# Block-causal attention and gated MLP on one core: the MLP over 9 blocks of 512 tokens in place of 16 half batches of 288

## The chip, the core and the metric

The kernel runs on one NeuronCore of a Trainium2 chip. The core has five engines that run side by side, each with its own queue that it works off in order: TensorE (PE in the profile; its weight loads are listed as PEld), VectorE (DVE), ScalarE (ACT), GpSimd (POOL) and SyncE (SP), which here issues the DMAs. Semaphores tie them together. SBUF is the working memory of 128 partitions; PSUM takes the results of TensorE, in banks of 2 KB a partition, which is 512 numbers in f32.

The metric is the time of one execution on the device in microseconds (us), less is better. Before the change it is 994.98 us, the median of three runs (994.43, 994.98, 995.88).

## The reference

What is computed, cut to what matters:

```python
# attention: batch 8, heads 8, sequence 576, head size 64
scores = (q @ k^T) / 8
scores = where(block_i >= block_j, scores, -1e9)     # blocks of 64 positions
attn = exp(scores - rowmax); attn = attn / (rowsum + 1e-9)
x = (attn @ v)  ->  [4608 tokens, 512]               # 8 batches x 576 tokens, heads side by side
# gated MLP without a nonlinearity
a = x @ w1                                           # 512 x 1024
b = x @ w2                                           # 512 x 1024
out = ((a * b) @ w3) @ w_out                         # 1024 x 1024, 1024 x 512
```

All inputs and the output are f32.

## The kernel before

**Work and tiling.** The 64 heads are worked off as 32 pairs (`n` from 0 to 31, four pairs to a batch; channel `c` of `x` is the pair's place in its batch). `pair(n)` computes attention for the two heads `j` of a pair and leaves `x` of that pair, transposed: 128 channels by 576 tokens. The products w3 @ w_out are taken once at the start, so the MLP is two products with w1 and w2 and one with the joined weight. Every operand of the MLP is split in a high and a low part (`w1h`/`w1l`, `xh`/`xl`, `gh`/`gl`) in the type fp32r, and a product is three matmuls: high x high, low weight x high, high weight x low.

**Stages.** In the first stage (pairs 0 to 3, `EARLY`) the weights are loaded, rebuilt from 64-bit words and split; attention of the first batch runs between these steps. Then the pool of that stage is closed, the pool `late` is opened over its memory, and pairs 4 to 31 run with the MLP of earlier batches woven in. After the last pair what is left of the MLP runs alone.

**The MLP before.** `gen_moe(b)` is a generator. For each half `h` of 288 tokens it goes over eight tiles `f` of the hidden size: 12 matmuls for `a`, 12 for `b`, both into PSUM tiles of the pool `ps_m` (two banks), then a copy of `a` by ACT, the product `g` by DVE, its high part by ACT and its low part by POOL. Then it goes over four tiles `e` of the output, 24 matmuls each, an ACT copy and an output DMA. Each `yield` ends a piece of 6 matmuls, so a batch has 96 pieces.

**The order.** TensorE's order is set by hand (`manual_schedule` for PE, from pair 4 on): the two strings of `PLAN`, one for each head, are worked off letter by letter. S is a tile of scores with its exponentials, V a piece of attention times v, M a piece of the row maxima of the next pair (`shift_mask`: casts, then six groups of matmuls with maxima on DVE, then a transpose), B and A the steps that split q and k (B for the second head of this pair, A for the first head of the next), R the row sums, N the taking of the result out of PSUM, T the division by the row sums, Q the split of v and the next load, F one piece of the MLP. Each pair has 24 F. `DELAY` is the number of F left out at the start of pair 4. The order on the other engines is left to the framework, which also adds the waits.

**Buffers that matter.** `raws` holds two buffers of 1792 numbers a partition, q, k and v of a pair together; `load(n + 2)` is called at the Q of the second head of pair `n`. `finish_x` splits each finished `x` at once into `xh` and `xl`, in halves of 288 tokens, in rotating buffers (eight in `xpool`, four in `late`); the subtraction for `xl` is on DVE for pairs 0 to 3 and on POOL later. Scores have two PSUM tiles (`ps_s`), the attention result one of two banks (`ps_x`), and the small products two (`ps_q`).

**Lines that the steps below speak of.** L182 are the mask matmuls `mx`, L186 their maxima, L233 the score matmuls, L248 and L249 the exponentials, L251 the low halves of the exponentials, L254 the row-sum additions on POOL, L296 attention times v, L309 the row sums' reduction `part`, L313 the small matmul `tot` that adds them over partitions, L160 the casts of q, k and v, L210 and L223 their low parts, L343 and L344 `xh` and `xl`, L392 the matmuls of `a` and `b`, L397 to L401 the steps of `g`, L408 the matmuls of the output, L412 and L413 its copy and DMA, L369 the product of the weights, L358 its low part, L96 the load of q, k and v.

Of the kernel before, what the change touches and what calls it, by code (L numbers as in the profile page):

```python
# [26 lines left out]
HALF = S // 2  # L27
RAW = 2 * S + 640
# [15 lines left out]
    "B F B S S F F B S S F F F F S M M F V V F V V F F R V F Q N F",  # L44
    "M A S F S F A S M F M S F F S M F A M V V V F F V V N Q R T M F F F",
# [7 lines left out]
DELAY = 3  # L53
# [5 lines left out]
def block_causal_attention__then__gated_mlp_kernel(ctx, tc, qkv, consts, ident_in, w1, w2, w3t, wout, out_t):  # L59
# [30 lines left out]
    raw_of = {}  # L90

    def load(n):
        t = raws.tile([P, RAW], F32, tag="raw", name=f"raw{n}")
        parts = (slice(S, 2 * S), slice(0, S), slice(2 * S, RAW)) if n == 0 else (slice(0, RAW),)
        for cols in parts:
            nc.sync.dma_start(out=t[:, cols], in_=qkv[n // NPAIR, n % NPAIR][:, cols])  # L96
        raw_of[n] = t

    load(0)
    nc.sync.dma_start(out=both, in_=ident_in)  # L100
    cst = raws.tile([P, RAW], F32, tag="raw", name="cst")
    nc.sync.dma_start(out=cst[0:D, 0 : 2 * S], in_=consts)
    for j in range(2):
        nc.vector.tensor_copy(qk[j][oth[j], 1::2, :], cst[0:D, 0 : 2 * S].rearrange("p (t s) -> p t s", t=2))
    nc.gpsimd.memset(qd, 0.0)

    tl = {}

    def open_early(pool):
        tl["early"] = pool  # L110
        tl["wo"] = pool.tile([P, NF, DM], F32, name="wo")

    def open_late():
# [4 lines left out]
        tl["pl"] = pool.tile([P, PW], F32R, name="pl")  # L118
# [45 lines left out]
    def shift_mask(n):  # L164
        r = raw_of[n]
        rqk = r[:, 0 : 2 * S].rearrange("p (t s) -> p t s", t=2)
# [34 lines left out]
    def prep_qk(n, j):  # L201
        rqk = raw_of[n][:, 0 : 2 * S].rearrange("p (t s) -> p t s", t=2)
# [10 lines left out]
    def prep_v(n, j):  # L213
        rv = raw_of[n][:, 2 * S :].rearrange("p (j c d) -> p j c d", j=2, c=5)[:, j]
# [10 lines left out]
    def s_tile(n, j, parts, p_early):  # L225
# [10 lines left out]
        for c, ks, at, q0, q1 in todo:  # L236
# [7 lines left out]
            if c == 0:  # L244
                p32 = rsum[:, q0:q1]
            else:
                p32 = tl["late"].tile([P, 448], F32, tag="p32", name=f"p{n}_{j}", bufs=2)[ks, 0:w]
# [76 lines left out]
    def take(n, j, xps, x32):  # L324
        o, x = own[j], oth[j]
        xl = tl["late"].tile([P, S], F32, tag="xlow", name=f"xlow{n}_{j}")
# [3 lines left out]
    def norm(n, x32, rr):  # L330
# [3 lines left out]
        nc.vector.tensor_tensor(out=x32, in0=x32, in1=rb, op=ALU.mult)  # L334

    def finish_x(n, x32):
        for h in range(2):
            at = (2 * n + h) % 12
            pool, bufs = (xpool, 8) if at < 8 else (tl["late"], 4)
            xh = pool.tile([P, HALF], F32R, tag="xh", name=f"xh{n}_{h}", bufs=bufs)  # L340
            xl = pool.tile([P, HALF], F32R, tag="xl", name=f"xl{n}_{h}", bufs=bufs)
            src = x32[:, h * HALF : (h + 1) * HALF]
            nc.scalar.copy(xh, src)  # L343
            (nc.vector if n < EARLY else nc.gpsimd).tensor_tensor(out=xl, in0=src, in1=xh, op=ALU.subtract)  # L344
            x_of[n // NPAIR, n % NPAIR, h] = (xh, xl)
# [35 lines left out]
    def gen_moe(b):  # L381
        mp, gh, gl = tl["late"], tl["gh"], tl["gl"]
        for h in range(2):
            for f in range(NF):
                acc = []
                for a, b2 in ((w1h, w1l), (w2h, w2l)):
                    t = ps_m.tile([P, 512], F32, tag="psm", name="ab")
                    fs = slice(f * P, (f + 1) * P)
                    for c in range(NC):
# [3 lines left out]
                        if c == 1 or (c == NC - 1 and len(acc) == 0):  # L393
                            yield
# [153 lines left out]
```

## Time and profile before

| what | value |
|---|---|
| three timed runs | 994.43, 994.98, 995.88 us |
| span of the profiled execution | 992.5 us |
| mean granted TensorE clock in it | 0.991 |
| first score matmul of pair 4 | 138.4 us |
| first MLP matmul | 142.1 us |
| last piece of the MLP woven into the pairs ends | about 912 us |
| last matmul starts | 988.5 us |
| moved by DMA over the span | 80.4 MB, 81 GB/s in the mean |

One execution is recorded by the hardware profiler, on the core's own clock. Its page gives the busy time of each engine, the span in 40 slices with one digit for the busy tenths of each, and the chain of work that ended last, followed back from the last instruction to what released it. Other views show the same record as groups of instructions by line, in order of time, or summed over windows. A matmul row such as `ab<-xh,w1h 128*128 128x288` names output and inputs, the size of the weight tile, and the moving tile (partitions x columns). Matmuls overlap in the pipeline: the duration of one is longer than the distance to the next, so the distance between starts is what to read. In an execution on one core there is no other core to disturb it.

### The profile page before, as it was taken

To read this page: it belongs to the slowest core of one execution; us is meant where nothing else is said; L and a number is where in the kernel's file an instruction comes from. 1 tells how busy PE (TensorE), PEld (TensorE's weight loads), DVE (VectorE), ACT (ScalarE), POOL (GpSimd) and SP (SyncE) were. 2 spreads that over 40 slices of the span, in tenths; PEclk is the share of its full clock that TensorE was granted. 3 is DMA by queue.
4 is the path that set the end of the run, shared out by engine and by line. 5 is a ranking of instruction groups with operands and counts; after the bars stand their busy time and mean duration, and the time that the engine had idled before them with its cause. 6 is when DMAs were issued, how large, how long until landed. Compare 5 with 4: busy or idle time off the path is not lost.

```text
span 992.5 us, 18182 instructions
## 1 busy us (share of the span) xinstructions
PE 960.8 (97%) x6624; PEld 879.1 (89%) x6624; DVE 695.6 (70%) x1316; ACT 557.2 (56%) x1433; POOL 535.6 (54%) x525
## 2 busy tenths in 40 slices
PE   4799979999999999999999999999999999999998
PEld 2355559999999999999999999999999999999998
DVE  7899997776777777777777777777767777774100
ACT  4656766555655556555655656665566555553221
POOL 0000027677675857676766767576776758572211
PEclk9799989999999999999999999999999999999999
DMA  7877622212222221211212222222122222100000
GB/s 239 260 256 233 196 62 63 54 57 74 62 68 80 63 85 51 85 54 47 72 59 77 63 86 62 74 62 60 52 74 65 65 81 62 49 13 25 7 19 25
DMA packets 36698, 80.40 MB, mean 81 GB/s; under 512 B 4416, under 2 KB 20928, under 8 KB 36608
## 3 DMA queue, kind: packets, MB, share of 16 engines
q1 hardware_dynamic: 36608, 79.23, 27.0%
q8 instruction: 52, 0.85, 0.3%
q14 instruction: 38, 0.31, 0.1%
HBM read 50.76 MB, written 9.44 MB: 61 GB/s over the span
## 4 chain that ended last, share of the span: by engine, by line
PE 83%; DVE 12%; DMA 2%; ACT 1%; issue 1%; SPq 0%; DVEq 0%; ACTq 0%
PE ab L392 38%; PE o L408 21%; PE s L233 10%; PE x L296 7%; PE mx L182 3%; PE w L369 3%; DVE m L186 2%; DVE qk L160 2%; DVE wbits L141 1%; DVE part L309 1%; DVE pl L251 1%; DMA raw<-in_qkv 1%; DVE qk L210 1%; PE tot L313 1%; DMA wraw<-in_w 1%
## 5 line engine op out<-in xcount | busy, mean ns | idle before, releaser
L254 POOL TENSOR_TENSOR rsum<-rsum,p 128x448 f32<-128x448 f32 x224 | 185.7, 829 | 135.9 <-ACT p L248 125.1
L401 POOL TENSOR_TENSOR gl<-g,gh 128x288 fp32r<-128x288 f32 x128 | 115.4, 902 | 114.5 <-ACT gh L400 110.2
L233 PE MATMUL s<-qk 128*128 128x288 f32 (+4 forms) x768 | 162.8, 317 | 13.8 <-DMA qk<-qk 4.6
L251 DVE TENSOR_TENSOR pl<-p,ph 128x448 fp32r<-128x448 f32 x168 | 138.8, 834 | 38.8 <-ACT ph L249 36.5
L392 PE MATMUL ab<-xh,w1h 128*128 128x288 f32 x512 | 158.7, 310 | 0.0
L408 PE MATMUL o<-gh,wh 128*128 128x288 f32 x512 | 155.3, 303 | 0.0
L392 PE MATMUL ab<-xh,w2h 128*128 128x288 f32 x512 | 154.0, 301 | 0.0
L392 PE MATMUL ab<-xl,w1h 128*128 128x288 f32 x512 | 151.5, 296 | 0.0
L392 PE MATMUL ab<-xh,w1l 128*128 128x288 f32 x512 | 151.4, 296 | 0.0
L408 PE MATMUL o<-gh,wl 128*128 128x288 f32 x512 | 151.1, 295 | 0.0
L392 PE MATMUL ab<-xh,w2l 128*128 128x288 f32 x512 | 151.0, 295 | 0.0
L392 PE MATMUL ab<-xl,w2h 128*128 128x288 f32 x512 | 150.9, 295 | 0.0
L408 PE MATMUL o<-gl,wh 128*128 128x288 f32 x512 | 150.8, 294 | 0.0
L210 POOL TENSOR_TENSOR qk<-raw,qk 64x1152 fp32r<-64x1152 f32 x54 | 144.1, 2668 | 2.0
L233 PEld LDWEIGHTS s<-qk 128*128 128x128 f32 (+1 forms) x768 | 114.9, 183 | 32.5 <-ACT pe L241 6.9
L186 DVE TENSOR_REDUCE m<-mx 128x1 f32<-128x512 f32 (+6 forms) x320 | 133.5, 452 | 10.6 <-PE mx L182 8.7
L223 POOL TENSOR_TENSOR vs<-raw,vs 128x320 fp32r<-128x320 f32 x56 | 49.7, 887 | 160.8 <-ACT vs L160 160.8
L249 ACT ACTIVATE ph<-s 128x288 fp32r<-128x288 f32 x336 | 130.7, 390 | 0.0
L399 DVE TENSOR_TENSOR g<-ab,a 128x288 f32<-128x288 f32 x128 | 58.2, 454 | 103.1 <-PE ab L392 66.6
L400 ACT CAST gh<-g 128x288 fp32r<-128x288 f32 x128 | 55.3, 432 | 110.7 <-DVE g L399 110.7
L248 ACT ACTIVATE p<-s 128x448 f32<-128x448 f32 x224 | 85.3, 381 | 50.8 <-PE s L233 36.1
L251 DVE TENSOR_TENSOR pl<-rsum,ph 128x288 fp32r<-128x288 f32 x112 | 60.4, 558 | 71.5 <-ACT ph L249 71.5
(70 smaller groups left out, 2136.9 us busy)
## 6 DMA issues: line engine op xcount, KB each, us to landing
raw<-in_qkv SPq DMA_DIRECT2D x31, 896.0 KB
qk<-qk SPq DMA_DIRECT2D x64, 288.0 KB
out_t<-o SPq DMA_DIRECT2D x64, 144.0 KB
wraw<-in_w3t SPq DMA_DIRECT2D x16, 512.0 KB
wraw<-in_w SPq DMA_DIRECT2D x16, 512.0 KB
wraw<-in_wout SPq DMA_DIRECT2D x8, 512.0 KB
qk<-ms SPq DMA_DIRECT2D x64, 2.2 KB
raw<-in_qkv SPq DMA_DIRECT2D x2, 288.0 KB
```

The costliest lines, as they stand in the source:

```text
L186: nc.vector.reduce_max(m[:, col : col + 1], sc, axis=AX.X)
L210: (nc.vector if n <= EARLY else nc.gpsimd).tensor_tensor(out=low, in0=rqk[o], in1=high, op=ALU.subtract)
L233: nc.tensor.matmul(t[ks, at : at + q1 - q0], qk[j][:, 2 + s, kr], qk[j][:, s, q0:q1], start=(s == 0), stop=(s == 1))
L248: nc.scalar.activation(p32, t[ks, at : at + w], AF.Exp, scale=SCALE)
L249: nc.scalar.activation(ph[ks, o : o + w], t[ks, at : at + w], AF.Exp, scale=SCALE)
L251: nc.vector.tensor_tensor(out=low, in0=p32, in1=ph[ks, o : o + w], op=ALU.subtract)
L254: nc.gpsimd.tensor_tensor(out=r, in0=r, in1=p32, op=ALU.add)
L296: nc.tensor.matmul(xps[:, to : to + w], v[:, c, :], parts[s][:, a : a + w], start=(u < 2 and s == 0), stop=((u, s) in ((0, 1), (len(PV) - ...
L392: nc.tensor.matmul(t[:, 0:HALF], l[:, c, fs], r, start=(c == 0 and s == 0), stop=(c == NC - 1 and s == 2))
L399: nc.vector.tensor_tensor(out=g32, in0=acc[1][:, 0:HALF], in1=a32, op=ALU.mult)
L401: nc.gpsimd.tensor_tensor(out=gl[:, f, :], in0=g32, in1=gh[:, f, :], op=ALU.subtract)
L408: nc.tensor.matmul(t[:, 0:HALF], l[:, f, es], r[:, f, :], start=(f == 0 and s == 0), stop=(f == NF - 1 and s == 2))
```

## The change

The MLP's unit becomes a block `k` of 512 tokens, counted over all 4608 tokens without regard to batches: 9 blocks, 96 pieces each, a piece being 3 matmuls of 512 columns. Block `k` takes tokens of batches `k - 1` and `k` (blocks 1 to 7), of batch 0 alone (block 0) or batch 7 alone (block 8); blocks 7 and 8 both need the last batch.

- `norm` multiplies `x` by the reciprocal row sums in two pieces, into f32 tiles per block and channel (`x_of[k, c]`, two buffers for each channel). `finish_x` is gone. `split_ready` splits a whole 512-token tile into `xh[c]` (ACT) and `xl[c]` (POOL), which have one buffer each; it is called when a pair is finished and when the last `f` of a block has been issued (`st["free"]`).
- In `gen_moe` the first `f` of a block takes the last channel last. `a * b` is written over `a32`; `o32` has one buffer.
- Raw inputs are two tiles, q and k (`rqk`) and v (`rv`). From pair 4 on each has one buffer. q and k of pair `n + 1` are loaded after the second B of pair `n`, v of pair `n + 2` at Q. Odd early pairs use the early pool, where the constants lie in the buffer that pair 1 takes after them.
- `PLAN`: the first head has one M less and one F more, the second one M more and one F less; `DELAY` is 6.
- Small tiles are cut: `pl`, two single buffers for `p32`, and `take` uses the tile `tr`.

```diff
-HALF = S // 2
-RAW = 2 * S + 640
+TB = 512
+NTB = NT // TB
+RQK, RV = 2 * S, 640
 PLAN = (
-    "B F B S S F F B S S F F F F S M M F V V F V V F F R V F Q N F",
-    "M A S F S F A S M F M S F F S M F A M V V V F F V V N Q R T M F F F",
+    "B F B S S F F B S S F F F F S M F F V V F V V F F R V F Q N F",
+    "M A S F S F A S M F M S F M S F M A M V V V F F V V N Q R T M F F F",
 )
-DELAY = 3
+DELAY = 6
...
-    raws = ctx.enter_context(tc.tile_pool(name="raws", bufs=2))
+    raws = ctx.enter_context(tc.tile_pool(name="raws", bufs=1))
-    xpool = ctx.enter_context(tc.tile_pool(name="xpool", bufs=8))
+    xpool = ctx.enter_context(tc.tile_pool(name="xpool", bufs=2))
...
+    def raw_pool(n):
+        return tl["early"] if n < EARLY and n % 2 else raws
+
+    def load_qk(n):
+        t = raw_pool(n).tile([P, RQK], F32, tag="rqk", name=f"rqk{n}")
+        for cols in (slice(S, 2 * S), slice(0, S)) if n == 0 else (slice(0, RQK),):
             nc.sync.dma_start(out=t[:, cols], in_=qkv[n // NPAIR, n % NPAIR][:, cols])
+        rqk_of[n] = t
+
+    def load_v(n):
+        t = raw_pool(n).tile([P, RV], F32, tag="rv", name=f"rv{n}")
+        nc.sync.dma_start(out=t, in_=qkv[n // NPAIR, n % NPAIR][:, RQK:])
+        rv_of[n] = t
...
-        tl["gh"] = pool.tile([P, NF, HALF], F32R, name="gh")
-        tl["gl"] = pool.tile([P, NF, HALF], F32R, name="gl")
+        tl["xh"] = [pool.tile([P, TB], F32R, name=f"xh{c}") for c in range(NC)]
+        tl["xl"] = [pool.tile([P, TB], F32R, name=f"xl{c}") for c in range(NC)]
+        tl["gh"] = pool.tile([P, NF, TB], F32R, name="gh")
+        tl["gl"] = pool.tile([P, NF, TB], F32R, name="gl")
...
-        nc.vector.tensor_tensor(out=x32, in0=x32, in1=rb, op=ALU.mult)
+        b, c = divmod(n, NPAIR)
+        for k in (b, b + 1):
+            lo, hi = max(k * TB, b * S), min((k + 1) * TB, (b + 1) * S)
+            if (k, c) not in x_of:
+                x_of[k, c] = xpool.tile([P, TB], F32, tag=f"x{c}", name=f"xr{k}_{c}")
+            sl = slice(lo - b * S, hi - b * S)
+            nc.vector.tensor_tensor(out=x_of[k, c][:, lo - k * TB : hi - k * TB], in0=x32[:, sl], in1=rb[:, sl], op=ALU.mult)
+        done_x.add((b, c))
+        split_ready()
+
+    def split_ready():
+        k = st["free"]
+        for c in range(NC):
+            if "xh" in tl and k < NTB and (min(k, B - 1), c) in done_x and (k, c) not in st["split"]:
+                st["split"].add((k, c))
+                src = x_of[k, c]
+                nc.scalar.copy(tl["xh"][c], src)
+                nc.gpsimd.tensor_tensor(out=tl["xl"][c], in0=src, in1=tl["xh"][c], op=ALU.subtract)
...
+    def gen_moe(k):
+        mp, xh, xl, gh, gl = tl["late"], tl["xh"], tl["xl"], tl["gh"], tl["gl"]
+        sides = ((w1h, w1l), (w2h, w2l))
+        for f in range(NF):
+            fs = slice(f * P, (f + 1) * P)
+            acc = [ps_m.tile([P, TB], F32, tag="psm", name="ab") for _ in sides]
+            order = [(i, c) for i in range(2) for c in range(NC)]
+            if f == 0:
+                order.sort(key=lambda ic: (ic[1] == NC - 1, ic))
+            for i, c in order:
+                a, b2 = sides[i]
+                for s, (l, r) in enumerate(((a, xh), (b2, xh), (a, xl))):
+                    nc.tensor.matmul(acc[i], l[:, c, fs], r[c], start=(c == 0 and s == 0), stop=(c == NC - 1 and s == 2))
+                if (i, c) == (0, NC - 1):
+                    a32 = mp.tile([P, TB], F32, tag="a32", name="a32", bufs=2)
+                    nc.scalar.copy(a32, acc[0])
+                if (i, c) != order[-1]:
+                    yield
+            nc.vector.tensor_tensor(out=a32, in0=acc[1], in1=a32, op=ALU.mult)
+            nc.scalar.copy(gh[:, f, :], a32)
+            nc.gpsimd.tensor_tensor(out=gl[:, f, :], in0=a32, in1=gh[:, f, :], op=ALU.subtract)
+            if f == NF - 1:
+                st["free"] = k + 1
+                split_ready()
+            yield
+        for e in range(DM // P):
+            t = ps_m.tile([P, TB], F32, tag="psm", name="o")
+            es = slice(e * P, (e + 1) * P)
             for f in range(NF):
+                for s, (l, r) in enumerate(((wh, gh), (wl, gh), (wh, gl))):
+                    nc.tensor.matmul(t, l[:, f, es], r[:, f, :], start=(f == 0 and s == 0), stop=(f == NF - 1 and s == 2))
+                if f < NF - 1:
+                    yield
+            o32 = mp.tile([P, TB], F32, tag="o32", name="o32")
+            nc.scalar.copy(o32, t)
+            nc.sync.dma_start(out=out_t[es, k * TB : (k + 1) * TB], in_=o32)
+            yield
...
                     elif step == "B":
                         fill(own_qk, 1)
+                        steps_b += 1
+                        if steps_b == 2 and n >= EARLY and not last:
+                            load_qk(n + 1)
...
-                        if j == 1 and n + 2 < NN:
-                            load(n + 2)
+                        if j == 1 and n + 2 <= EARLY:
+                            load_qk(n + 2)
+                        if j == 1 and n + 2 < NN and n + 1 != NPAIR:
+                            load_v(n + 2)
...
-    mlp = (None for b in range(B - 1) for _ in gen_moe(b))
+    mlp = (None for k in range(NTB) for _ in gen_moe(k))
     for n in range(NPAIR, NN):
         pair(n)
     fill(mlp, 1000)
-    fill(gen_moe(B - 1), 1000)
```

More of the change, by code (lines that the diff above doesn't have):

```diff
@@ L88, in block_causal_attention__then__gated_mlp_kernel, with open_early @@
     oth = [slice(D, P), slice(0, D)]
[L90 to L99, printed above, removed]
-    nc.sync.dma_start(out=both, in_=ident_in)
-    cst = raws.tile([P, RAW], F32, tag="raw", name="cst")
-    nc.sync.dma_start(out=cst[0:D, 0 : 2 * S], in_=consts)
+    tl = {}
+    rqk_of, rv_of = {}, {}
+    def raw_pool(n):
[3 more added lines that the diff above has]
+        for cols in (slice(S, 2 * S), slice(0, S)) if n == 0 else (slice(0, RQK),):
+            nc.sync.dma_start(out=t[:, cols], in_=qkv[n // NPAIR, n % NPAIR][:, cols])
+        rqk_of[n] = t
[3 more added lines that the diff above has]
+        rv_of[n] = t
+    load_qk(0)
+    load_v(0)
+    nc.sync.dma_start(out=both, in_=ident_in)
+    wstack = ExitStack()
+    wp = wstack.enter_context(tc.tile_pool(name="wp", bufs=1))
+    tl["early"] = wp
+    cst = wp.tile([P, RQK], F32, tag="rqk", name="cst")
+    nc.sync.dma_start(out=cst[0:D], in_=consts)
     for j in range(2):
-        nc.vector.tensor_copy(qk[j][oth[j], 1::2, :], cst[0:D, 0 : 2 * S].rearrange("p (t s) -> p t s", t=2))
+        nc.vector.tensor_copy(qk[j][oth[j], 1::2, :], cst[0:D].rearrange("p (t s) -> p t s", t=2))
     nc.gpsimd.memset(qd, 0.0)
[L107 to L111, printed above, removed]
+    def open_early():
+        tl["wo"] = wp.tile([P, NF, DM], F32, name="wo")
     def open_late():
@@ L201, in prep_qk @@
     def prep_qk(n, j):
-        rqk = raw_of[n][:, 0 : 2 * S].rearrange("p (t s) -> p t s", t=2)
+        rqk = rqk_of[n].rearrange("p (t s) -> p t s", t=2)
         o, x = own[j], oth[j]
@@ L246, in s_tile @@
             else:
-                p32 = tl["late"].tile([P, 448], F32, tag="p32", name=f"p{n}_{j}", bufs=2)[ks, 0:w]
+                p32 = tl["late"].tile([P, 448 if c % 2 else 320], F32, tag=f"p32{c % 2}", name=f"p{n}_{j}")[ks, 0:w]
             nc.scalar.activation(p32, t[ks, at : at + w], AF.Exp, scale=SCALE)
@@ L325, in take @@
         o, x = own[j], oth[j]
-        xl = tl["late"].tile([P, S], F32, tag="xlow", name=f"xlow{n}_{j}")
+        xl = work.tile([P, S], F32, tag="tr", name=f"xlow{n}_{j}")
         nc.scalar.copy(xl[o], xps[x, 384:960])
@@ L333, in norm @@
         nc.vector.transpose(rb, rr.unsqueeze(2).broadcast_to([P, S // 32, 32]))
-        nc.vector.tensor_tensor(out=x32, in0=x32, in1=rb, op=ALU.mult)
[L336 to L345, printed above, removed]
+        b, c = divmod(n, NPAIR)
[7 more added lines that the diff above has]
+        split_ready()
+    done_x = set()
+    st = {"free": 0, "split": set()}
+    def split_ready():
[6 more added lines that the diff above has]
+                nc.gpsimd.tensor_tensor(out=tl["xl"][c], in0=src, in1=tl["xh"][c], op=ALU.subtract)
     def gen_w(wp):
@@ L428, in block_causal_attention__then__gated_mlp_kernel @@
         prep_v(0, j)
-    load(1)
+    load_qk(1)
+    load_v(1)
     weights = gen_w(wp)
```

49 lines of the change are left out of this document (7 added, 42 removed).

## The prediction

> **What bounds the kernel now.** I read the page first (busy shares, the span in 40 slices, the chain that ended last by line), then the chain in order of time, then the windows of one pair of heads in the steady part.
>
> ```profile
> span 992.5 us, 18182 instructions
> ...
> PE 960.8 (97%) x6624; PEld 879.1 (89%) x6624; DVE 695.6 (70%) x1316; ACT 557.2 (56%) x1433; POOL 535.6 (54%) x525
> ...
> PE   4799979999999999999999999999999999999998
> ...
> DVE  7899997776777777777777777777767777774100
> ...
> PE 83%; DVE 12%; DMA 2%; ACT 1%; issue 1%; SPq 0%; DVEq 0%; ACTq 0%
> ```
>
> TensorE is busy 97% of the span and holds 83% of the chain; from the seventh slice to the last but one it never falls under nine tenths. VectorE has its nines only in the first six slices, 149 us (weights). The three timed runs (994.43 to 995.88, median 994.98) lie about 2.5 us over this span of 992.5; I take that as fixed, so the sum below is a change added to 994.98.
>
> A busy PE is pipelined, so what counts is the distance from one matmul to the next. The chain in order of time gives it: the last batch's MLP alone, and one row of the weight product.
>
> ```profile
> 52.93 6.87 PE w L369 x16
> ...
> 495.96 3.18 PE ab L392 x24
> ...
> 523.47 3.20 PE o L408 x24
> ...
> 912.48 25.28 PE ab L392 x192
> 937.76 12.80 PE o L408 x96
> 950.56 25.50 PE ab L392 x192
> 976.06 12.79 PE o L408 x96
> ```
>
> The last four rows are 576 matmuls of 288 columns in 76.37 us: 132.6 ns each, with nothing else on the engine. The first row is 16 matmuls of 512 columns in full f32, 429 ns each. If those stream their columns twice, a column costs 0.419 ns, 288 columns 120.8 ns, and 11.8 ns of each 288-wide matmul are not streaming. That remainder is what the change can save.
>
> The steady part repeats per pair of heads: the rows at 495.96 and 523.47 are the same place in two pairs, 27.5 us apart. Windows over one pair (first head, second head up to the row sums' matmul, the rest); columns: length, then busy us of PE, PEld, DVE, ACT, POOL:
>
> ```profile
> 471.40:484.40 13.00, 13.00 (x98) 12.80 (x96) 8.05 (x12) 7.31 (x21) 9.17 (x9) 1.00 0.38 115
> 484.40:495.40 11.00, 10.97 (x82) 10.22 (x80) 9.56 (x21) 7.93 (x21) 7.88 (x7) 1.00 0.12 27
> 495.40:499.10 3.70, 3.66 (x28) 3.67 (x29) 3.09 (x8) 1.69 (x5) 2.02 (x3) 1.00 0.01 1
> ```
>
> PE is full throughout, but in the second head VectorE has only 1.44 us left of 11.00. There the chain leaves PE:
>
> ```profile
> 490.61 0.30 PE s L233 x4
> ...
> 490.93 1.23 DVE qk L160
> ...
> 493.87 0.36 DVE g L399
> ...
> 494.70 0.68 DVE part L309
> ...
> 495.44 0.41 PE tot L313 x2
> ```
>
> From the last score tile to the row-sum matmul the work of VectorE (a cast of the next pair, the low halves, the maxima, `g`, the sums) takes as long as PE's own work. VectorE is nearly the bound here; over the whole pair it is not (20.7 of 27.7 us).
>
> **The change part by part.**
>
> *Wider matmuls.* Before there are 16 half batches x 288 matmuls (per `f` 2 x 4 x 3, eight `f`; per `e` 8 x 3, four `e`) = 4608 of 288 columns; after, 9 x 288 = 2592 of 512. The columns are the same, 1.327 million. Before: 4608 x 132.6 ns = 611 us. No 512-wide fp32r matmul is in the trace; the nearest is the 448-wide one of P·V:
>
> ```profile
> 492.66 0.36 PE L296 MATMUL x<-ph,vs 128*128 128x448 f32 x1
> 492.86 0.36 PE L296 MATMUL x<-pl,vs 128*128 128x448 f32 x1
> 493.06 0.31 PE L296 MATMUL x<-ph,vs 128*128 128x320 f32 x1
> ...
> 507.40 0.37 PE L296 MATMUL x<-pl,vs 128*128 128x448 f32 x1
> 507.61 0.29 PE L392 MATMUL ab<-xh,w1h 128*128 128x288 f32 x1
> ```
>
> Starts are 0.20, 0.20 and 0.21 us apart. A line through 132.6 at 288 and 200 at 448 gives 227 ns at 512; the 0.21 pulls it up. I take 228: 2592 x 228 = 591 us, **-20 us**. Bounds: 214.7 ns (half of 429) gives 556 us, -55; the old cost per column (132.6/288 = 0.4604, x 512 = 235.7) gives 611, nothing gained.
>
> The Trainium skill, "TensorE: Matmul & The Clock Gate", section "Back-to-back issue gap", puts the gap of a warm matmul at N/2.4 + 2.5 ns. The f32 row agrees (1024/2.4 + 2.5 = 429); the 288-wide row doesn't (122.5 against 132.6 measured), so I don't sum by it. By the page's figures the MLP would go from an estimated 564 to 559 us, only 5 us gained, while 215.8 ns set against the measured 611 us would be a gain of 52.
>
> *The second head's balance.* A step F of the mixed order issues 6 matmuls (0.796 us) before and 3 (0.684 us) after; each pair has 24 either way. But PLAN gives the second head one F less and one mask group M more. Up to the row sums PE has 8 F before and 7 after: 11.00 - 8 x 0.796 + 7 x 0.684 + 0.23 (the mask matmul) = 9.65 us. VectorE's work there (a row of the chain, where a 512-wide maximum holds VectorE 0.60 us, and two groups by line):
>
> ```profile
> 98.79 0.60 DVE m L186
> ```
>
> ```profile
> L399 DVE TENSOR_TENSOR g<-ab,a 128x288 f32<-128x288 f32 x128 | 58.2, 454 | 103.1 <-PE ab L392 66.6 <-PE x L296 19.8 <-issue 16.1
> ...
> L358 DVE TENSOR_TENSOR wl<-w,wh 128x512 fp32r<-128x512 f32 x8 | 5.5, 684 | 1.8 <-ACT wh L357 1.8
> ```
>
> 9.56, plus 0.60 for the maximum that moved in, minus two `g` of 0.454, plus one of 512 columns out of PSUM (0.684, as `wl`) = 9.94 us. That is 0.29 more than PE's 9.65: PE, whose order is fixed by hand, would wait about 0.3 us at the row sums' matmul, with the final mask transpose and three F queued behind it. I take 0.35, a little over the balance as PE waits some already: 28 pairs x 0.35 = **+10 us**. Bounds: 0, if work slides into the 5.6 us that VectorE has free beside this stretch (4.95 in the first head, 0.61 behind); 28 x 1.1 = +31, if half of today's 1.44 us of gaps stay.
>
> *ACT and POOL in the steady part* get fewer, wider instructions and have 3 us of room in each head.
>
> ```profile
> L401 POOL TENSOR_TENSOR gl<-g,gh 128x288 fp32r<-128x288 f32 x128 | 115.4, 902 | 114.5 <-ACT gh L400 110.2
> ...
> L254 POOL TENSOR_TENSOR rsum<-rsum,p 128x448 f32<-128x448 f32 x56 | 64.3, 1149 | 112.0 <-ACT p L248 107.8 <-DVE m L186 3.1 <-DVE g L399 1.1
> ...
> L344 POOL TENSOR_TENSOR xl<-x,xh 128x288 fp32r<-128x288 f32 x56 | 44.1, 808 | 28.6 <-ACT xh L343 28.6
> L344 DVE TENSOR_TENSOR xl<-x,xh 128x288 fp32r<-128x288 f32 x8 | 3.4, 453 | 0.5 <-ACT xh L343 0.5
> ```
>
> A 512-wide POOL subtraction is about 1.149 x 512/448 = 1.3 us (estimate from the L254 row). `xh`/`xl` now have one buffer and are rewritten when the last `f` of a block is through: three channels at once, 3.9 us of POOL once in four pairs. Behind it wait the `rsum` additions of the next pair. But the block then has its `o` part before it reads them, 32 F steps or more than a pair, and the fourth channel is read last in the first `f`. Hidden: 0; if POOL's spare time failed, at most 3.9 us x 8 = +31.
>
> *Raw q, k with one buffer.* The load of the next pair waits for POOL's subtraction of this pair's second head. The timeline of POOL, of SP and of VectorE, and a window (its last two columns are the DMA share and GB/s):
>
> ```profile
> 493.08 2.66 POOL L210 TENSOR_TENSOR qk<-raw,qk 64x1152 fp32r<-64x1152 f32 x1
> ```
>
> ```profile
> 498.49 0.40 SPq L96 DMA_DIRECT2D raw<-in_qkv  x1
> ```
>
> ```profile
> 504.00:506.00 2.00, 2.00 (x18) 1.97 (x17) 1.58 (x4) 0.43 (x2) 1.89 (x2) 1.00 0.00 0
> ```
>
> ```profile
> 505.93 0.74 DVE L160 CAST qk<-raw 64x1152 fp32r<-64x1152 f32 x1
> ```
>
> The subtraction ends at 495.75. Today's load of 896 KB, issued at 498.5, is over by 504, 5.5 us; 576 KB should take under 5. So the data would be there at about 501, and the cast that reads it into `qk` runs at 505.93. Some 5 us are left, 4 in a pair of 25: cost 0. Without that cover each us is 28 us in all. On SP's queue the load goes behind the copy of the second head's `qk`; the row-maximum copies and output stores behind it are not due for several us.
>
> *The early part* (VectorE-bound). Eight `xl` of 0.453 leave VectorE, 3.6 us; the split multiplication by `rb` adds four small instructions. **-3 us** (bounds -4, and +1 as the second raw load now waits for the constants' buffer).
>
> *The hand-over.* The first F is put off by 6 steps, not 3, and four 512-wide `xh` copies and `xl` subtractions stand ahead of pair 4.
>
> ```profile
> 140.64 1.65 PE s L233 x4
> 142.28 4.77 PE ab L392 x24
> ```
>
> The first 24 MLP matmuls take 4.77 us instead of 3.2: the clock is still low. Three F less to fill the wait for exponentials, 3 x 0.8 us: **+2.5** (bounds 0 and +6). *The tail* holds two blocks, not one batch, but that is PE alone in both, already counted; the last output is 512 wide, +0.3.
>
> Sum: -20 + 10 - 3 + 2.5 + 0.3 = -10, so 985.
>
> **The rivals.** *VectorE becomes the bound of the second head* (slower side). One mechanism: it needs 9.94 us plus the gaps it can't lose against PE's 9.65. For: 9.56 of 11.00 busy already, and the chain through it. Against: 4.95 us free in the first head. The wait per pair from which it cancels the gain is (20 + 3 - 2.5 - 0.3)/28 = 0.7 us. At 1.0: -20 + 28, 1003.
>
> *The overhead of a matmul mostly vanishes at 512* (215 to 216 ns). For: 11.8 ns over streaming now. Against: at 448 it is still about 12. It gives -52, but PE's stretch in the second head shrinks to 11.00 - 6.37 + 7 x 0.647 + 0.23 = 9.39 and VectorE's excess grows to 0.55: with 0.6 a pair, -52 + 17 = -35, 960. The gap of the Trainium skill ("TensorE: Matmul & The Clock Gate", "Back-to-back issue gap") has this value at 512, but it fails at 288, so it gets no more than the 0.10 below.
>
> *The change doesn't do what it says:* cost goes with columns, 235.7 ns. For: the 0.21 after a 448. Nothing is saved; PE's stretch is 9.8 and the wait 0.2: +5, 1000.
>
> *The raw load comes late* because SP holds it behind waiting copies: 1 us a pair, 1013. Against: the 5 us above.
>
> **How the numbers follow.** Forecast 0.52 (its own range 974 to 994), VectorE 0.20, overhead gone 0.10, per column 0.11, raw load 0.07. The likeliest gives 985. The low end 960 takes in the second rival, the high end 1004 the first and third; what lies outside is the raw load, some of the first rival beyond 1.0 us, and the far end of the second. About 0.2% (2 us) is what a measurement of this kernel can tell from no change. Faster: 0.49 of the forecast, 0.10, and 0.06 of the first and third, 0.65; same 0.09; slower 0.26.
>
> **What would show it.** In the chain's last rows, 512-wide groups: 192 matmuls in 43.8 us for 228 ns (41.2 at the bound, 45.3 per column). The step from one pair to the next: 27.5 - 24 x 0.112 + 0.35 = 25.2 us. Windows of the second head: VectorE over 95% busy, and a wait of `tot` for VectorE. The first MLP matmul near 142 us. Waits of ACT or VectorE for the raw load should be absent after the first pairs. The forecast is wrong if the 448 rows mislead about 512, or if the order of VectorE's instructions shifts, which no row of before can show.

## The result, and the profile after

The changed kernel takes 1101.15 us (median of four runs, 1099.04 to 1103.43) against 994.78 us of the kernel before on the same chip: a ratio of 1.106, with an interval of 1.104 to 1.108. I had forecast 985 us in a range of 960 to 1004. The profiled execution has a span of 1097.3 us. One run further down, the one with the copies first, was profiled in an execution of 1025.07 us that stands apart from its other three (1008.1 to 1010.1), so its time is taken from those three. The page of after, in the same parts as shown of before:

```profile
span 1097.3 us, 13914 instructions
...
PE 988.5 (90%) x4608; PEld 763.6 (70%) x4608; DVE 777.6 (71%) x1284; ACT 535.6 (49%) x1265; POOL 527.3 (48%) x449
...
PE   4799978989988898899999898899889988999998
...
PE 60%; DVE 28%; ACT 6%; issue 5%; DMA 1%; SPq 0%; ACTq 0%; DVEq 0%
```

TensorE now shows eights all over the part with attention, and its share of the chain fell from 83% to 60%, while VectorE's rose from 12% to 28%. The loss is in the pairs, not in the MLP alone. The last rows of after's chain, 512-wide groups:

```profile
962.38 43.85 PE ab L412 x192
1006.23 21.77 PE o L430 x96
...
1071.90 21.77 PE o L430 x96
```

192 matmuls in 43.85 us are 228.4 ns each, 96 in 21.77 us are 226.8: the 228 ns forecast for the wider matmuls. But a pair, which I had put at 25.2 us, takes 29.4 us (mean distance of the `mt` transposes from pair 6 on; 27.55 before). 28 pairs x 4.2 us are 118 us, and 985 + 118 = 1103: all of the miss lies in the pairs.

The windows of one pair's two heads in after (columns as before), the second from the first score tile of that head to the row sums' matmul:

```profile
491.50:506.65 15.15, 15.15 (x75) 12.27 (x73) 9.38 (x16) 8.71 (x22) 7.98 (x8) 1.00 0.30 87
506.65:519.60 12.95, 10.26 (x55) 7.71 (x54) 12.40 (x21) 6.54 (x17) 7.96 (x8) 1.00 0.18 42
```

In the second head VectorE is busy 12.40 of 12.95 us and TensorE idles 2.7. Three timelines show its end: VectorE's, POOL's and TensorE's (L171 are the casts, L220 their low parts, L261 the low halves of the exponentials, L196 the mask maxima).

```profile
513.87 0.76 DVE L171 CAST qk<-rqk 64x1152 fp32r<-64x1152 f32 x1
514.66 0.36 DVE L261 TENSOR_TENSOR pl<-p,ph 128x192 fp32r<-128x192 f32 x1
515.05 2.57 DVE L261 TENSOR_TENSOR ph<-p,ph 64x64 fp32r<-64x64 f32 x1
517.66 1.22 DVE L196 TENSOR_REDUCE m<-mx 128x1 f32<-128x320 f32 x4
```

```profile
514.71 2.83 POOL L220 TENSOR_TENSOR qk<-rqk,qk 64x1152 fp32r<-64x1152 f32 x1 [0.70 <-DVE qk L171]
```

```profile
519.61 0.41 PE L323 MATMUL tot<-part,ident 128*128 128x36 f32 x2 [1.64 <-DVE m L198]
```

A subtraction of 64x64 elements lasts 2.57 us. It ends at 517.62, and POOL's subtraction, begun 0.34 us before it, at 517.54. In the kernel before the same two ran the other way round: `ph` first, in VectorE's timeline, and POOL's subtraction at 493.08, as the prediction shows it. There POOL was still busy with the row-sum additions up to 493.00; in after it is done with them early, idles 0.70 us until VectorE's cast ends, and so starts its subtraction ahead of `ph`.

```profile
492.86 0.23 DVE L251 TENSOR_TENSOR ph<-p,ph 64x64 fp32r<-64x64 f32 x1
```

The groups with one shape each, of before and of after:

```profile
L251 DVE TENSOR_TENSOR ph<-p,ph 64x64 fp32r<-64x64 f32 x56 | 20.6, 368 | 1.8
```

```profile
L261 DVE TENSOR_TENSOR ph<-p,ph 64x64 fp32r<-64x64 f32 x56 | 80.4, 1435 | 1.9 <-ACT ph L259 0.2
```

These are means over both heads. Taken apart, the 27 instructions of the second heads from pair 4 on last 0.23 us each before and 2.57 us each after.

Behind the wait at `tot` the granted clock falls. After's chain behind one such wait, and 7 us later in the same pair, and a window over the first of the two (the third number from the end is the granted clock):

```profile
285.06 4.34 PE ab L412 x12
...
292.02 2.75 PE ab L412 x12
```

```profile
285.00:290.00 5.00, 5.00 (x18) 4.02 (x17) 4.66 (x8) 2.99 (x6) 1.44 (x2) 0.66 0.34 105
```

The same 12 matmuls take 1.6 us more. Of the 26 steps from pair to pair from pair 5 on, 16 show this (29.6 to 29.9 us, a granted clock of 0.94 over the pair) and ten do not (28.4 to 29.2 us, 1.00), though the wait is the same in all. The mean clock is 0.966 against 0.991. The waits of after also show one that was to be absent:

```profile
PEld tot L323 <- DVE m L198: 47.2, 27, 1.7
```

```profile
ACT kb L171 <- DMA rqk<-in_qkv: 20.8, 23, 1.8
```

### The profile page after: what moved, and what is told of

It is laid out like the page before. It is cut to its first block, busy times and chain, and to the rows that moved or that the text cites. A ratio compares the mean times of both kernels' runs of the same rounds, so it can differ in the third digit from the quotient of the medians.

```text
span 1097.3 us, 13914 instructions
## 1 busy us (share of the span) xinstructions
PE 988.5 (90%) x4608; PEld 763.6 (70%) x4608; DVE 777.6 (71%) x1284; ACT 535.6 (49%) x1265; POOL 527.3 (48%) x449
## 4 chain that ended last, share of the span: by engine, by line
PE 60%; DVE 28%; ACT 6%; issue 5%; DMA 1%; SPq 0%; ACTq 0%; DVEq 0%
PE ab L412 28%; PE o L430 16%; DVE m L196 7%; DVE ph L261 6%; PE s L243 6%; DVE pl L261 5%; PE x L306 4%; PE w L388 3%; DVE qk L171 2%; ACT rsum L258 2%; DVE part L319 2%; ACT ph L259 1%; PE tot L323 1%; DVE qk L220 1%; DVE wbits L152 1%
## 5 line engine op out<-in xcount | busy, mean ns | idle before, releaser
L243 PE MATMUL s<-qk 128*128 128x288 f32 (+4 forms) x768 | 164.1, 320 | 17.4 <-ACT ph L259 5.3
L261 DVE TENSOR_TENSOR pl<-p,ph 128x448 fp32r<-128x448 f32 x168 | 152.6, 922 | 37.7 <-ACT ph L259 36.1
L220 POOL TENSOR_TENSOR qk<-rqk,qk 64x1152 fp32r<-64x1152 f32 x54 | 148.4, 2748 | 18.3 <-DVE qk L171 18.2
L196 DVE TENSOR_REDUCE m<-mx 128x1 f32<-128x512 f32 (+6 forms) x320 | 129.8, 446 | 5.0 <-PE mx L192 3.6
L412 PE MATMUL ab<-xh,w1h 128*128 128x512 f32 x288 | 126.1, 438 | 0.1
L430 PE MATMUL o<-gh,wh 128*128 128x512 f32 x288 | 120.7, 419 | 0.0
L412 PE MATMUL ab<-xh,w2h 128*128 128x512 f32 x288 | 118.9, 413 | 0.0
L412 PE MATMUL ab<-xh,w1l 128*128 128x512 f32 x288 | 118.1, 410 | 0.0
L412 PE MATMUL ab<-xl,w1h 128*128 128x512 f32 x288 | 118.0, 410 | 0.0
L430 PE MATMUL o<-gh,wl 128*128 128x512 f32 x288 | 116.6, 405 | 0.0
L430 PE MATMUL o<-gl,wh 128*128 128x512 f32 x288 | 116.2, 403 | 0.0
L412 PE MATMUL ab<-xl,w2h 128*128 128x512 f32 x288 | 114.7, 398 | 0.0
L412 PE MATMUL ab<-xh,w2l 128*128 128x512 f32 x288 | 114.1, 396 | 0.0
L192 PE MATMUL mx<-kb,qd 128*128 128x512 bf16 (+6 forms) x320 | 73.6, 297 | 25.4 <-DVE m L196 18.1
```

Of the source, the lines that this page charges most:

```text
L192: nc.tensor.matmul(sc, qd[:, i, :], kb[:, a:b], start=True, stop=True)
L196: nc.vector.reduce_max(m[:, col : col + 1], sc, axis=AX.X)
L220: (nc.vector if n <= EARLY else nc.gpsimd).tensor_tensor(out=low, in0=rqk[o], in1=high, op=ALU.subtract)
L243: nc.tensor.matmul(t[ks, at : at + q1 - q0], qk[j][:, 2 + s, kr], qk[j][:, s, q0:q1], start=(s == 0), stop=(s == 1))
L261: nc.vector.tensor_tensor(out=low, in0=p32, in1=ph[ks, o : o + w], op=ALU.subtract)
L412: nc.tensor.matmul(acc[i], l[:, c, fs], r[c], start=(c == 0 and s == 0), stop=(c == NC - 1 and s == 2))
```

## The experiments

Two suspects came out of the traces. *The hold* (the expectations call it blocking): POOL's subtraction holds VectorE's `ph`, because the new `PLAN` made VectorE late in the second head. Its own rival is *load*: VectorE simply has too much work there. *The raw loop*: subtraction, load into the one buffer, ScalarE's casts of the next pair, its exponentials, the scores, and so to the next subtraction. The rival to all of these is that wide blocks cost the time by themselves. The kernel before was timed beside each group of runs (medians of 995.0 to 996.0 us). The expectations call the two strings of `PLAN` the list of due places.

### The list of due places and the hold

**`ph` on POOL.** The changed kernel, with

```diff
-            nc.vector.tensor_tensor(out=low, in0=p32, ...)
+            (nc.gpsimd if c == 4 and j == 1 else nc.vector).tensor_tensor(out=low, in0=p32, ...)
```

> The changed kernel, but the low half of the last score tile of the second head (L261, 64x64) is taken by GpSimd, ahead of its 2.7 us subtraction for the next pair, and no longer by VectorE. Blocking theory: in the changed kernel this 64x64 instruction holds VectorE for 2.57 us in every pair because GpSimd's subtraction (L220) started first; without it the row-sum matmul comes about 2.3 us earlier in each of 28 pairs (64 us), and the clock no longer falls after a wait of over 2 us (another 15 to 25 us): 1010 to 1025. Load theory (VectorE simply has too much work in the second head since a mask group moved in and an F moved out): only 0.25 us of work leaves a head, 28 x 0.25 = 7 us: about 1094.

1078.59 us (ratio 1.084, 1.081 to 1.087), 23 us less by one instruction of 64x64; the wait at `tot` is gone and the clock is back at 0.990. The load rival had only 7 us for this. But the pair is still 28.6 us, so the hold is not all of the loss.

**POOL's subtraction of the second head in four pieces.**

```diff
+        step = S if n <= EARLY or j == 0 else S // 4
+        for a in range(0, S, step):
-            ...tensor_tensor(out=low, in0=rqk[o], in1=high, op=ALU.subtract)
+                ...tensor_tensor(out=low[:, :, a : a + step], in0=rqk[o][:, :, a : a + step], in1=high[:, :, a : a + step], op=ALU.subtract)
```

> The changed kernel, but GpSimd's subtraction for the second head (64x1152) is issued as four of 64x288. Blocking theory, held for one whole instruction: VectorE's 64x64 instruction then waits 0.7 us at most, not 2.3; 1.6 us a pair and the fallen clock come back: 1025 to 1050. If the two engines shared the bandwidth instead, the four pieces would slow VectorE as one does: 1100. Load theory: 1100 or a little more, as GpSimd has three more starts.

1107.54 us (ratio 1.112, 1.109 to 1.115), a loss where the theory of the hold had a gain:

```profile
L263 DVE TENSOR_TENSOR ph<-p,ph 64x64 fp32r<-64x64 f32 x56 | 30.5, 546 | 1.9 <-ACT ph L261 0.2
```

`ph` fell from 1435 to 546 ns in the mean (0.72 us in the second heads, where it was 2.57), so the hold lasts one instruction of POOL; but the four pieces take 3.27 us in place of 2.83, and ScalarE's wait for the raw load rose from 20.8 to 93.1 us.

**The old list, and the new list alone.** The changed kernel with the two strings of `PLAN` of before; and the kernel before with those of after, nothing else.

> The changed kernel with the order strings of the kernel before: one mask group and one F go back (13 F in the first head, 11 in the second). Load theory: VectorE loses 0.6 us of work in the second head and TensorE gains 0.46 there, so the wait at the row sums goes: 25.5 to 26 us a pair, 1000. Blocking theory: VectorE is about 1 us less late; if that is not enough to be ahead of GpSimd's subtraction, the 2.3 us stay: 28 to 28.5 us a pair, 1065 to 1085; if it is enough, all goes: 1000.

> The kernel before (16 half batches of 288) with the order strings of the changed kernel and nothing else. Load theory: in the second head TensorE has 11.00 - 0.80 + 0.23 = 10.4 us, VectorE 9.56 + 0.60 = 10.2 and some gaps: 0 to 0.5 us a pair, 995 to 1010. Blocking theory: the same unless VectorE comes to its 64x64 instruction after GpSimd has begun the subtraction; then 2.3 us a pair and more, 1050 to 1070.

1076.02 us (ratio 1.081, 1.078 to 1.083), and 1100.17 us (ratio 1.104, 1.101 to 1.107). With the old list `ph` lasts 0.23 us in every second head again. Moving one mask group into the second head and one F out of it costs the kernel before 105 us without any wide block. Its chain shows the same held subtraction:

```profile
511.35 2.58 DVE ph L251
...
513.96 1.22 DVE m L186 x4
```

So there are two limits: the list alone gives 1100, all the rest of the change 1076, both together 1101. The larger hides the other, and taking one away gives back 25 us only. The runs of the changed kernel from here on start from the old list; where one moves letters in it, that is said. The chain of the changed kernel with it, over the second limit:

```profile
508.00 2.64 POOL qk L220
...
510.66 3.60 DMA rqk<-in_qkv
...
514.28 0.67 ACT kb L171
...
516.08 0.67 ACT qd L171
...
516.77 0.41 ACT rsum L258
...
517.53 1.17 PE s L243 x4
```

Subtraction, load, casts, exponential, scores, one after another with no slack: the raw loop.

### The raw loop

**One raw buffer in the kernel before**, its half batches, its list and its `DELAY` kept.

> The kernel before (16 half batches of 288, its own list of due places), with one thing of the change: one late buffer each for the raw q,k and the raw v, and the loads asked for after the second head's B. Theory of the raw loop (subtraction 2.64 us, load 3.6 us, then ScalarE's casts, which stand ahead of the exponentials, then the scores): the loop of 28.3 us a pair in the changed kernel with the old list, plus 16 instructions of 0.107 us that the old split put on ScalarE, gives about 30 us a pair and 1064 us (1045 to 1075), with ScalarE's casts waiting for the raw load by 3 us or more. Rival (the raw load is hidden and the wide blocks cost the time): 995 us, within 5.

1060.16 us (ratio 1.067, 1.063 to 1.070), 30.1 us a pair: as the loop's theory had it. The single buffer alone costs 65 us.

**q and k in two tiles; ScalarE's order written out.** Two attempts to shorten the loop in the changed kernel:

> The changed kernel with the old list of due places, the raw q and k in two tiles, so that k is cast, subtracted and loaded anew while q is being subtracted. Theory of the raw loop: the loop becomes some 2.6 us shorter, 25.7 us a pair, 1003 us (995 to 1010), and ScalarE's wait for the raw load goes under 1.5 us a pair. Rival (the loop is not what binds, the wide blocks do): 1076 us, unchanged.

> The changed kernel with the old list of due places, and ScalarE's order written out as TensorE's is, so that the casts of the next pair's k and q stand where the program puts them, behind the exponentials of the heads before, and not ahead of them. Theory of the raw loop through ScalarE's order: most of the 4.1 us that the casts wait for the load no longer hold up the exponentials, 25 to 25.8 us a pair, 990 to 1010 us. Rival (the load is late whatever ScalarE's order, since the row-maximum copies stand behind it in the queue of SP): 1060 to 1076 us.

1087.39 us (ratio 1.093) and 1258.55 us (ratio 1.264): both misses. With two tiles the q half is still loaded only after the whole subtraction, and ScalarE waits 110.5 us for it in all; the hold is back too, 1.33 to 1.46 us at 17 places, as POOL's subtraction now comes in two pieces. With ScalarE in program order the casts go behind the exponentials, but everything else of its order changes too (TensorE's mask matmuls now wait 105.6 us for its casts), so this run doesn't speak on the loop.

**No loads of q and k from pair 5 on.**

> The changed kernel with the old list of due places; the raw q and k of pairs 5 to 31 are not loaded, and the values of pair 4 are used again, so that the loads are left out. Theory of the raw loop: with the wait for the load gone the wide blocks show what they are worth, 24.9 to 25.2 us a pair, 980 to 988 us. Rival (the wide blocks themselves cost the time): over 1050 us.

998.1 us (ratio 1.003, 1.002 to 1.004), 25.56 us a pair. With the load gone 78 us of 81 are gone; wide blocks themselves cost next to nothing. But they gain nothing either: 13 us over my forecast, though the loads are left out.

**The casts later.** Two ScalarE instructions of two columns write zeros into the places of the casts and read the last weights of the first head, so the casts can't be put ahead of that head's exponentials. In the first string, shown against the old list, both M go to the end of the head with them:

```diff
+        if n > EARLY:
+            late = tl["ph"][:, PC[3] : PC[3] + 2].bitcast(F32)
+            nc.scalar.mul(out=kb[:, 0:2], in_=late, mul=0.0)
+            nc.scalar.mul(out=qd[:, 0, 0::BLK], in_=late, mul=0.0)
         cast(n, kb, rqk[:, 1, :], CAST[1])
-    "B F B S S F F B S S F F F F S M M F V V F V V F F R V F Q N F",
+    "B F B S S F F B S S F F F F S F V V F V V F F M R V F Q N M F",
```

> The changed kernel with the old list of due places and its loads, but ScalarE's casts of the next pair's raw k and q stand behind the last exponentials of the first head and not ahead of its first: two ScalarE instructions of two columns write zeros into their places, read from the last weights of that head, and so hold the casts back; the first two mask steps of the list go to the end of the first head. Theory of the raw loop (the load is late only for a reader that stands too early in ScalarE's order): ScalarE's wait for the raw load all but goes, the pair takes 25.5 to 25.9 us as without the loads, 996 to 1008 us. Rival (the load is late for the later readers too, or SP's queue holds the row-maximum copies behind it): over 1050 us.

1038.51 us (ratio 1.043, 1.041 to 1.045): 37.5 us back, about half of what the theory wanted. ScalarE no longer waits for the load. The chain shows what is late now (the copy `qk<-ms` brings the row maxima into `qk`), and the waits have its sum:

```profile
515.14 2.63 POOL qk L224
...
517.79 0.34 SPq L100
...
518.22 3.53 DMA qk<-ms
...
521.80 0.66 PE s L247 x3
```

```profile
PE s L247 <- DMA qk<-ms: 34.1, 28, 2.2
```

SP's queue holds the load (L100) until the subtraction ends, and the copy, issued 0.43 us behind it, releases the scores 3.53 us later. My prediction had named this queue and said that the copies were not due for several us.

**More cover in the second head.** One F goes from ahead of the last score tile to behind it.

> As the run before, and in the second head one F is moved from ahead of the last score tile to behind it, which puts 0.69 us more of TensorE's work between that tile and the row sums. If the 0.29 us by which the row sums' matmul waits for VectorE in each pair of the run without loads is the balance of the second head, it goes: 8 us less than the run before, 988 to 1000 us. Rival (VectorE starts later by as much, since the last scores come from a TensorE and ScalarE that are no earlier): within 3 us of the run before.

1046.6 us (ratio 1.052, 1.050 to 1.054): slower. The copies were still a limit (27.8 us of TensorE's waits), and the hold came back in every fourth pair, as VectorE's and POOL's timelines show:

```profile
464.52 2.59 DVE L265 TENSOR_TENSOR ph<-p,ph 64x64 fp32r<-64x64 f32 x1
```

```profile
464.35 2.69 POOL L224 TENSOR_TENSOR qk<-rqk,qk 64x1152 fp32r<-64x1152 f32 x1
```

Those six pairs take 28.4 to 28.7 us, where the run before has 26.2 to 26.4. So this settled nothing about VectorE's balance, but it shows that the race between the two is not over.

**The copies ahead of the load; the load in POOL's queue.** Both on the kernel with the casts later:

```diff
+        if n > EARLY:
+            nc.scalar.mul(out=t[0:NB, 0:2], in_=ms_of[n - 1][0:NB, 0:2].bitcast(F32), mul=0.0)
```

```diff
-            nc.sync.dma_start(out=t[:, cols], ...)
+            (nc.gpsimd if n > EARLY else nc.sync).dma_start(out=t[:, cols], ...)
```

> As the run with the casts later (1038.5 us), and in SP's queue the raw load stands behind the copies of the row maxima into qk, not ahead of them: a ScalarE instruction of 9x2 elements, read from the row maxima, is written first into the raw tile. In the run with the casts later that copy lands 3.5 us after its issue, 0.4 us behind the load of 576 KB in the same queue, and TensorE waits 2.2 us for it in each pair. Theory (what is left of the loss is that copy behind the load): the wait goes, the pair takes 25.6 us, 997 to 1006 us. Rival (the copy is late whatever stands ahead, since the subtraction and the maxima end late): 1030 us or more.

> As the run with the casts later, but the raw q,k of the pairs behind the first ones are loaded over a queue of GpSimd, whose own subtraction releases the buffer, and no longer over that of SP. If the copy of the row maxima is late because it stands behind the load in one queue, it comes in time: 997 to 1010 us, less what issuing the load costs GpSimd. Rival (the two transfers take the same 16 engines, so the copy is late in another queue too): 1030 us or more.

1009.02 us (ratio 1.014, 1.012 to 1.016) and 1061.49 us (ratio 1.067, 1.064 to 1.070). Putting the load behind the copies gives 29.5 us back. In another queue the copy is as late: SP issues it ahead of the load, and it still takes 3.72 us in the chain. The timelines of SP and of POOL, and the chain:

```profile
506.75 0.79 SPq L213 DMA_DIRECT2D qk<-ms  x1
```

```profile
506.95 0.57 POOL L100 DMA_DIRECT2D rqk<-in_qkv  x1 [0.41 <-POOL qk L224]
```

```profile
506.75 3.72 DMA qk<-ms
```

So 2.2 KB issued within 0.5 us of a load of 576 KB is late in whichever queue. By the copy's packets in the traces its last byte is moved 1.5 us after the issue in the kernel before, in the run without loads and in the run with the copies first, but 2.9 us after it behind the load and 3.0 us with the load in POOL's queue (medians). Issued 0.9 us behind the last copy, as in the run with the copies first, the load does little harm:

```profile
PE s L249 <- DMA qk<-ms: 3.9, 3, 2.2
```

In that trace `ph` is held again in four second heads (2.55 us; pairs of 28.5 to 28.8 us against 25.9), so the old second string alone doesn't end the race for good. Why the load in POOL's queue costs 23 us more than in SP's was not settled.

### What is left: VectorE in the second head

**`xh` of a block's last channel later; one F ahead of `tot`.** Both start from the run with the copies first. They leave out the new split of the last channel of block 7, so the time misses one copy and one subtraction.

> As the run with the copies first (1009.6 us), and ScalarE's copy xh of a block's last channel stands behind the last exponentials of the next pair's first head. In that run it stands ahead of the first exponentials and waits for the end of norm, one pair in four: there the chain goes from VectorE's xr to ScalarE's xh (542.74) to the exponentials and the scores (544.02). Theory (the single buffer of xh, which I had costed at nothing, costs some 2 us in one pair of four): 13 us less, 994 to 1000 us. Rival (something else makes that pair late, such as the norm itself): 1004 us or more.

> As the run with xh later, and one of the three F behind the row sums' matmul stands ahead of it, so that TensorE has 0.69 us of work while VectorE makes the row sums. If the balance of the second head still costs 0.3 to 0.6 us a pair there, it goes: 8 to 12 us less than the run with xh later, 984 to 992 us. Rival (the final maximum's transpose, now one F later, makes the copies of the row maxima late for the next pair's scores): no gain or a loss against that run.

1008.11 us (ratio 1.012, 1.010 to 1.014): the place of that copy of `xh` costs about 1 us, which the runs can't tell from nothing; my prediction had put it at nothing. 1028.25 us (ratio 1.031, 1.028 to 1.034): the wait at `tot` went, but the later transpose made the row-maximum copies late (TensorE waits 22.9 us for them), worst in one pair of four.

**The transpose first; a cast on ScalarE.** From the run with the copies first, `Q R T M F F F` becomes `Q M R F T F F` at the end of the second string; then also `CAST[0] or (n > EARLY and j == 0)` for the cast of the first head's q and k.

> As the run with the copies first (1009.6 us), with the end of the second head in another order: the transpose of the maxima, then one F, then the row sums' matmul, then two F (before: row sums' matmul, transpose, three F). VectorE has 0.69 us more for the row sums, and the copies of the row maxima are no later. Theory (VectorE is the bound of the second head and costs the 0.58 us that the row sums' matmul waits in each pair): 25.5 us a pair, 10 to 14 us less, 995 to 1000 us. Rival (the wait goes to the transpose, which waits for the maxima just ahead of the sums): 1004 us or more.

> As the run with the transpose first, and the cast of the next pair's first-head q,k, which takes VectorE 1.3 us in the second head, is ScalarE's and stands in the first head behind the other casts. Theory (VectorE is the bound of the second head): its waits there go too, 25.2 us a pair, 985 to 992 us. Rival (POOL's subtraction of that head now comes earlier, or ScalarE later, and something else takes the time): 1000 us or more.

1018.19 us (1006.49 to 1022.61, the profiled execution being the shortest; ratio 1.020, 1.017 to 1.024) and 1007.4 us (ratio 1.013, 1.011 to 1.015): no gain. The wait went from `tot` to the transpose (14.6 us in 23 pairs, 18.1 in the second run). I had moved the wrong cast. The chain of that second run:

```profile
525.80 1.33 DVE qk L173
...
528.09 1.22 DVE m L202 x4
529.30 0.69 DVE part L325
...
530.08 0.28 PE mt L206
```

The cast ahead of the maxima and sums is that of the next pair's second head, which the framework pulls forward.

**That cast on ScalarE, and then `ph` on POOL too**, both from the kernel with the copies first:

```diff
-        cast(n, high, rqk[o], CAST[0])
+        cast(n, high, rqk[o], CAST[0] or (n > EARLY and j == 1))
```

> As the run with the copies first (1009.6 us), and the cast of the next pair's second-head q,k is ScalarE's (the run with ScalarE's cast moved the one of the first head, which was not at the end of the chain). In the runs so far that cast holds VectorE 1.33 us between the last score tile and the row sums. Theory (VectorE is the bound of the second head, and the rest of the loss): the 0.58 us wait at the row sums' matmul goes, 25.2 to 25.4 us a pair, 987 to 996 us. Rival (POOL's subtraction starts earlier too and holds VectorE's low halves, or ScalarE's cast makes its copies of the second head late): 1003 us or more.

> As the run with the second head's cast on ScalarE, and the 64x64 low half of the second head's last tile is POOL's, ahead of its subtraction, so that this subtraction can't hold it on VectorE. If the subtraction, now earlier, holds VectorE's ph there, this run is faster than that one, by 1 us a pair or more; if not, the two agree within 5 us.

999.7 us (ratio 1.0045, 1.003 to 1.006) and 999.19 us (ratio 1.0036, 1.002 to 1.005). Nine us back, and no wait at `tot` in the pairs; the two agree, and `ph` lasts 0.37 us at most in the second heads of the first of them, so POOL's subtraction holds nothing there. This is the best that I found with wide blocks and all the work done, and it is still 4 us slower than the kernel before.

## Why the prediction was wrong, step by step

**Wider matmuls, -20: right where they run alone.** 228.4 and 226.8 ns were measured for 228 forecast. Woven into the pairs the 72 MLP matmuls of a pair take 17.4 us up to the next matmul's start in the best run, against 19.7 us for 144 before (from the starts in the two traces): 2.3 us gained, not 24 x 0.112 = 2.7.

**The second head's balance, +10: the first step that failed.** I summed VectorE's durations to 9.94 us, weighed them against TensorE's 9.65, and took 0.35 us a pair. The place was right, and the first rival had named it, but not the mechanism: both took the durations as fixed. That of `ph` isn't: it depends on whether it starts before or after POOL's 2.7 us subtraction. In before it started first, by 0.2 us. With the new list VectorE was late, POOL came first, and 0.23 us became 2.57. With the clock that falls behind the wait this is 3.9 us a pair in the run with the list alone (31.5 against 27.55) and 105 us in all, where I had 0.35 and 10. The Trainium skill ("SBUF — State Buffer", "Who interferes with whom") says that a VectorE instruction with two SBUF inputs contends with a GpSimd instruction that reads SBUF, that the port pair they share is an exclusive lock, and that the order of issue decides who blocks; the trace agrees, by the 2.57 us that end 0.08 us after the subtraction, and by the 0.72 us that are left when it comes in four pieces. I had closed with the remark that a shift in VectorE's order would break the forecast. Around this instruction the order stayed (cast, `pl`, `ph`); what flipped was the race against POOL.

**Raw q, k with one buffer, cost 0: the second failed step.** "Some 5 us are left" was counted to VectorE's cast at 505.93. The first readers are ScalarE's casts, which stand ahead of the next head's exponentials in ScalarE's order, so by as much as the load is late the scores are late. With two buffers those casts never waited for a load in the pairs from 4 on, so no wait in the trace of before pointed to them; ScalarE's timeline shows their place:

```profile
492.15 0.67 ACT L160 CAST kb<-raw 128x576 bf16<-128x576 f32 x1 [0.26 <-PE mx L182]
```

This cast is for the mask matmuls that begin at 505.54, so it reads the same q and k as VectorE's cast at 505.93, and it runs before the subtraction that frees a single buffer has ended (495.75). At that place there was no cover at all. Alone the step costs 65 us (1060.16), 2.5 us a pair. Undone in the changed kernel it has two parts: 37.5 us by the casts' place and 29.5 us by the row-maximum copies that share the transfer's time with the load. My rival of the raw load put it at 1 us a pair with a chance of 0.07; its queue was the right one, but the load held the copies, not the copies the load.

**Hand-over, +2.5, and early part, -3.** The first MLP matmul starts at 145.2 us, not near 142: the four `xh` copies stand ahead of the first exponentials of pair 4. The transposes' step from pair 4 to 5 is 32.3 us against 30.1 before (29.5 in the best run), and the early part gave nothing back (pair 4's first transpose at 135.8 us against 135.0).

**How the 106 us go back.** The old list 25, the casts later 37.5, the copies first 29.5, the cast off VectorE 9 leave 999.7. Against the forecast of 985 the best run keeps 25.55 us a pair for 25.2, some 10 us, and 3.5 us of a later first MLP matmul. That last 0.35 us is about what the woven matmuls gain less than forecast: the pair's 25.55 us are 17.4 of MLP and 8.2 of the rest, against 19.7 and 7.9 before. Why they gain less wasn't settled: TensorE waits for no single thing there, and one pair in four is half a us longer, where `norm` and the split of a block fall.

**The gain that was to be had.** The kernel before kept TensorE full, so the 20 us were all there was, against costs of 9 to 37 us each that came with the new list and with the buffer given up for the room that wide blocks take. Those, and not the 228 ns, made the forecast wrong.

## What to carry to other kernels

Where an engine's instructions fit with a few tenths of a us to spare, look in the timelines at which of two contending engines starts first, and price the case in which the order flips; a sum of durations can't show it. And count such a race as won only where the trace of the new kernel shows it: the hold came back here in single pairs. Before a second buffer is given up, list every reader of the buffer in each engine's own order, what stands behind that reader, and what shares the transfer's time and queue. When a loss has several limits in series, undo them one after another and keep each undone: one alone gave 25 us of 106 and would have looked like a minor cause.

## What the runs showed of the hardware

A 64x64 subtraction on VectorE lasted 2.57 us in place of 0.23 where a POOL subtraction over 64x1152 had begun 0.3 us earlier, and 0.72 us where that came in four pieces. A copy of 2.2 KB issued within 0.5 us of a load of 576 KB took 3.5 us in the same queue behind it, and 3.7 us in another queue though issued 0.2 us ahead of it. Behind a wait of 1.6 us at one matmul, with another of 0.5 us just ahead of it, the granted clock was 0.66 over the next 5 us and 12 matmuls took 4.34 us in place of 2.75, in 16 of 26 pairs.
